# Filling up 64-row products, turning a block on TensorE, and moving weight sums to VectorE in a two-layer transformer kernel

## The chip, the cores and the metric

The kernel runs on one core of one Trainium2 chip. The core has five engines that run side by side, each with its own instruction queue: TensorE (PE, with its weight loader PEld), VectorE (DVE), ScalarE (ACT), GpSimd (POOL) and SyncE (SP, which here only issues transfers). Matrix products go from SBUF into the eight banks of PSUM, and DVE and ACT read them from there. DMA queues move data between DRAM and SBUF. The metric is device microseconds of one execution.

## The reference

Two layers, each an attention block and a gated block, on 2048 tokens of 448 features with 16 heads of 28:

```python
x = A_x
x = x + _A_ref(_layernorm(x, axis=-1), A_wqkv, A_wo)
x = x + _B_ref(_layernorm(x, axis=-1), B_w_gate, B_w_up, B_w_down)
x = x + _A_ref(_layernorm(x, axis=-1), A_wqkv, A_wo)
x = x + _B_ref(_layernorm(x, axis=-1), B_w_gate, B_w_up, B_w_down)
```

`_A_ref` is softmax attention, `(softmax(q k^T / sqrt(28)) v) wo`. `_B_ref` is `(sigmoid(x w_gate) * (x w_up)) w_down` with 1792 inner features. Both layers use the same weights. Inputs and output are float32.

## The kernel before

**Number format.** Products run on 16-bit pairs: a float32 operand is split into a high and a low float16 part, and a product is the sum of three 16-bit products (high x high, low x high, high x low). Splitting is one ACT cast (high) and one DVE subtraction (low). 448 features are three tiles of 128 rows and a tail of 64; in the tail, the high and low parts share one tile of 128 rows.

**Layer, stage by stage.** `project` makes queries, keys and values for four blocks of 512 tokens. `attend` runs the heads, `out_project` multiplies by `wo` and adds to `x`, `gated` runs the gated block. Engines follow the order in which the code issues instructions; each waits by semaphore for the tiles that it needs. SBUF tiles come from a ring of 19 large slots (`big`) and 12 quarter slots (`qrt`), first in, first out, so a new tile may wait for the last reader of an old one.

**Attention.** A unit is a score tile of 128 keys x 512 queries; a chunk is 128 keys against all 2048 queries, four units; a head has 16 chunks. Units go in groups of three: PE writes scores (L999) into three PSUM banks, ACT takes the exponential of the whole group (L1014), PE multiplies by the values two groups later (L1050) into an accumulator bank, one of two that alternate by head. At the end of a head `finish` copies the accumulator (L1076), divides and splits on DVE, and DMAs carry the result into `ot` (L1094 to L1097). A few units a head, set by `FEW` in the first layer and two otherwise, are taken from ACT: `score_aside` writes their scores into the other accumulator bank, which is free only after the previous head's copy at L1076, and DVE computes the exponential by a polynomial (nine operations, L1024 to L1033). `HeadOperands.load` loads a head's queries and keys from `qk_scr` on SP's queue; two rows of the key tile hold the constant `UNIT`, written by a DVE memset of 18 rows (L561) that comes first, and later DMAs overwrite all but two of them.

**Weights for later.** In the first layer's attention, `Prepare` reads `wo`, `w_gate`, `w_up` and `w_down`, measures them, splits them on DVE and writes the parts to DRAM (`o_parts`, `gu_parts`, `dn_parts`). Its steps are tied to chunk numbers: 12 measuring steps 4 chunks apart from chunk 6, then 5 splits 5 chunks apart, then 14 splits of gate or up weights, also 5 chunks apart. Reads, writes and the sums for the next split (`add_up`, L897) are POOL's: POOL's queue issues the DMAs, and POOL itself adds. Two large slots hold raw weights, two hold packs waiting to be written.

**Gated block.** The gate and up products use a seven-product scheme for 2 x 2 matrix halves: 256 of the features by 256 of the tokens and so on, so seven products do the work of eight. `half_steps` makes the seven moving operands of a 512-token block: four `wide` ones (two row tiles each) and three `short` ones (one row tile and a 64-row tail). In `of_halves` (L467 to L481) a wide operand gives six matmuls of 256 columns and a short one five, of which the last is over 64 rows. `gate_and_up` does one pair of inner tiles for gate and up on four PSUM banks, `chain` and `side`: 48 matmuls of wide and 30 of short operands. ACT copies the first three rounds out of the chain banks (L1278), DVE adds the side banks (L1294, L1301). The down products (`dnp`, L1247 to L1249) of the previous pair follow, 24 matmuls. An iteration is one pair of one block: 4 blocks x 7 pairs in each layer. Steps that prepare the next block are woven in by `run_fill`, one or two an iteration.

**Output projection.** `out_project` multiplies 16 token tiles by `wo` (11 matmuls each). Tiles 0 to 5 run their first nine matmuls ahead, since the last head's rows arrive late, then their last two; tiles 6 to 15 follow in bank t % 6. DVE adds each result to `x` (L1164). Between tiles the first gated block is prepared: `norm` (statistics on DVE, reciprocal root on POOL), `squares` (DVE scales and transposes in squares of 32), `store` and `gather` (the squares go to DRAM and come back with features on rows), then six empty steps, then the seven `half_steps`, the last three of which come after all tiles.

Of the kernel before, what the change touches and what calls it, by code (L numbers as in the profile page):

```python
# [13 lines left out]
F16 = mybir.dt.float16  # L14
# [5 lines left out]
P = 128  # L20
# [37 lines left out]
N_SUMS = 25  # L58
SHORT = ((10, 23, 12), (11, 24, 13), (8, 22, 9))

FEW = "1111010101"

N_SLOTS = 19
N_QUART = 12
# [38 lines left out]
def interleaved_layers(ctx: ExitStack, tc: tile.TileContext, x_in, wqkv, wo, w_gate, w_up,  # L103
# [31 lines left out]
    def bank(i, name):  # L135
        return psum(f"bank{i}", name, [P, 512])
# [100 lines left out]
    class Block:  # L237
# [10 lines left out]
        def __init__(self, b, halves=False):  # L248
            self.b = b
            self.halves = halves  # L250

        def norm(self, js=range(TB)):
            b = self.b
# [77 lines left out]
        def half_steps(self):  # L331
            def cut(k, t):

                return self.raw[:, k:k + 2, :].rearrange(
                    "p k (i t c) -> p k t i c", i=4, t=TB)[:, :, t:t + 2]

            def ordered(v):
                return v.rearrange("p k (t i c) -> p k t i c", t=2, i=4)

            def subtract(name, a, b):  # L340
                t = qrt.get(name, [P, 2, W // 2])
                a, b = [v if len(v.shape) == 5 else ordered(v) for v in (a, b)]
                for k in range(2):
                    nc.vector.tensor_tensor(ordered(t)[:, k], a[:, k], b[:, k],
                                            op=ALU.subtract)
                return t

            def divide(to, v):

                hi, lo = to[:, 0], to[:, 1]  # L350
                if len(v.shape) == 5:
                    for k in range(2):
                        nc.scalar.copy(ordered(hi)[:, k], v[:, k])
                        nc.vector.tensor_tensor(ordered(lo)[:, k], v[:, k], ordered(hi)[:, k],
                                                op=ALU.subtract)
                else:
                    nc.scalar.copy(hi, v)
                    nc.vector.tensor_tensor(lo, v, hi, op=ALU.subtract)  # L358

            def double(to):  # L360
                nc.scalar.copy(to[64:P, 0, 1], to[0:64, 0, 1])

            def r11():
                self.wide = big.get("xwide", [P, 4, 2, 2, W // 2], F16)
                self.short = big.get("xshort", [P, 3, 2, 2, W // 2], F16)
                self.t1 = subtract("t1", cut(0, 2), cut(0, 0))
                divide(self.wide[:, 0], cut(0, 0))

            def t1():
                self.t2 = subtract("t2", cut(2, 2), self.t1)  # L370
                divide(self.wide[:, 1], self.t1)
                qrt.put(self.t1)

            def t2():
                self.t3 = subtract("t3", cut(2, 2), cut(0, 2))
                divide(self.wide[:, 2], self.t2)

            def t3():
                self.t4 = subtract("t4", cut(2, 0), self.t2)
                divide(self.wide[:, 3], self.t3)  # L380
                qrt.put(self.t2, self.t3)

            def r21():
                divide(self.short[:, 0], cut(2, 0))
                double(self.short[:, 0])

            def t4():
                divide(self.short[:, 1], self.t4)
                double(self.short[:, 1])
                qrt.put(self.t4)  # L390

            def r22():
                divide(self.short[:, 2], cut(2, 2))
                double(self.short[:, 2])
                big.put(self.raw)

            return [r11, t1, t2, t3, r21, t4, r22]
# [8 lines left out]
        def begin(self):  # L406
            uid[0] += 1
            self.mv = cpool.tile([P, TB, 2], F32, name=f"mv_{uid[0]}", tag="mv", bufs=2)
            self.rs = cpool.tile([P, TB], F32, name=f"rs_{uid[0]}", tag="rs", bufs=2)
            self.xn = big.get("xn", [P, TB, D])  # L410
            self.turn_banks(4, range(4))

        def stats(self, j):
            st = cpool.tile([P, 6], F32, name=f"st_{uid[0]}_{j}", tag="st", bufs=4)
# [10 lines left out]
        def turn(self, j):  # L425
            for kt in self.pt:
                c = slice(kt * P, min((kt + 1) * P, D))
                nc.tensor.transpose(self.pt[kt][0:c.stop - c.start, j * P:(j + 1) * P],
                                    self.xn[:, j, c], ident)

        def turned_high(self):
            for kt, pt in self.pt.items():
# [34 lines left out]
    def of_halves(pm, w, blk, k, first):  # L467


        if k < 4:  # L470
            x = blk.wide[:, k]
            terms = [(w[:, i], x[:, j, t]) for t in range(2)
                     for i, j in ((2 * k + t, 0), (2 * k + t, 1), (14 + 2 * k + t, 0))]
        else:
            x = blk.short[:, k - 4]
            main, low, tail = SHORT[k - 4]
            terms = [(w[:, main], x[:, 0, 0]), (w[:, main], x[:, 1, 0]), (w[:, low], x[:, 0, 0]),
                     (w[:, tail], x[:, 0, 1]), (w[0:64, tail], x[0:64, 1, 1])]
        for i, (a, x) in enumerate(terms):
            nc.tensor.matmul(pm, a, x, start=(first and i == 0),  # L480
                             stop=(i == len(terms) - 1), skip_group_check=True)  # L481
# [64 lines left out]

    qk_scr = dpool.tile([2 * D, 2, S], F16, name="qk_scr")
    g_scr = dpool.tile([H, 2, S], F16, name="g_scr")

    class HeadOperands:  # L550

# [6 lines left out]

        def load(self):
            h, q, k = self.h, self.q, self.k  # L560
            nc.vector.memset(k[96:RG, :], UNIT)  # L561
            qs = qk_scr[h * DH:(h + 1) * DH]
            ks = qk_scr[D + h * DH:D + (h + 1) * DH]
            both = "d c n -> (d c) n"
# [22 lines left out]
    def project(layer, wq, first):  # L587
# [92 lines left out]

        def nothing():
            pass


        along = [tile0, tile1, tile2, lambda: wq.measure(2), lambda: wq.size(2), wq.split_v,
# [123 lines left out]
    class Prepare:  # L809


        def __init__(self):
            nc.vector.memset(sums[:, 3:7], 0.0)
            self.part = cpool.tile([P, 2], F32, name="part", tag="part", bufs=1)
            self.raws, self.packs = big.ring(2), big.ring(2)
            tiles = [("o", 0)] + [("d", j) for j in range(4)] + [("gu", j) for j in range(7)]
            order = [(self.measure, what) for what in tiles] + [
                (self.split, what) for what in tiles[:5] + [(w, p) for p in range(NP)
                                                            for w in ("g", "u")]]
            self.sums = self.ready_sums = None  # L820
            self.read(*tiles[0])
            self.steps = deque()
            at = 6
            for i, (do, what) in enumerate(order):
                then = order[i + 1][1] if i + 1 < len(order) else None
                self.steps.append((at, lambda do=do, what=what, then=then:
                                   self.step(do, what, then)))
                at += 4 if do == self.measure else 5
                if i == len(tiles) - 1:
                    self.steps.append((at, self.sizes))  # L830
            self.steps.append((at, self.end))
# [9 lines left out]
            big.free.extend(self.packs)  # L841

        def read(self, kind, j):
            self.next = big.at(self.raws, "raw", [P, 2048])
            if kind == "o":
                load_rows(self.view(self.next, kind), wo, 0, D, nc.gpsimd)
            elif kind == "gu":
# [25 lines left out]

        def step(self, do, what, then):
            raw = self.next
            if then:
                self.read(*then)
            self.write()
            self.sums = self.ready_sums
            if then and len(then[0]) == 1 and then[0] in "gu" and do == self.split:  # L880
                self.ready_sums = self.add_up(self.view(self.next, then[0]))
            do(raw, *what)

        def write(self):
            if self.pack:
# [3 lines left out]
        def add_up(self, v):  # L889
# [3 lines left out]
            for to, a, b, op in ((s12[:, 0], l21, l22, ALU.add),  # L893
                                 (s12[:, 1], s12[:, 0], l11, ALU.subtract),
                                 (s34[:, 0], l11, l21, ALU.subtract),
                                 (s34[:, 1], l12, s12[:, 1], ALU.subtract)):
                nc.gpsimd.tensor_tensor(to, a, b, op=op)  # L897
            return s12, s34

        def add(self, m, v):  # L900
# [24 lines left out]
        def split(self, raw, kind, j):  # L925
# [5 lines left out]
            elif kind in "gu":  # L931
                m = "gu".index(kind)
                t = big.at(self.packs, "pack", [P, N_SUMS, P], F16)
                s12, s34 = [a.rearrange("p a k n -> p (a k) n") for a in self.sums]
                for to, a in ((t[:, 0:2], v[:, 0:2, 0]), (t[:, 2:6], s12), (t[:, 6:10], s34),
                              (t[:, 10:14].rearrange("p (k z) n -> p k z n", k=2), v[:, 2:4])):
                    scaled_high(to, a, 4 + m, nc.vector)
# [4 lines left out]
                    scaled_low(to, hi, a, 4 + m)  # L942
                scaled_low(t[64:P, 9], t[0:64, 9], s34[0:64, 3], 4 + m)
                scaled_low(t[64:P, 12:14], t[0:64, 12:14], v[0:64, 3], 4 + m)
                qrt.put(*self.sums)
                self.pack = (gu_parts[j, m], t)
            else:
                n = self.count(j)
# [201 lines left out]
    def out_project(outs, gate):  # L1150
# [1 line left out]
        nc.scalar.activation(warm, warm, AF.Sigmoid)  # L1152
        nc.scalar.reg_load(gate_scale, back.bitcast(I32)[0:1, 3:4])
        first = Block(0, True)
        steps = first.steps()
        steps = deque(steps[:5] + [lambda: None] * 4 + steps[5:])
        early = 6

        def products(pm, t, kts):
# [10 lines left out]
        pms = [bank(t, "op")[:, 0:D] for t in range(early)]  # L1170
        for t in range(early):
            products(pms[t], t, range(3))
        for t in range(early):
            products(pms[t], t, [3])
            add(pms[t], t)
            if t >= TB - 1:
                run_fill(steps)
        for t in range(early, NT):
            pm = bank(t % 6, "op")[:, 0:D]
            products(pm, t, range(4))  # L1180
            add(pm, t)
            run_fill(steps)
        big.put(*outs.kt, gate.out)
        run_fill(steps, 9)
        return first
# [189 lines left out]
    keep_busy(14)  # L1375
    wq.measure(0)
    first.begin()
    first.parts()
    first.stats(0)
    first.stats(1)  # L1380
# [55 lines left out]
```

## Time and profile before

| | us |
|---|---|
| median of three runs | 2049.62 (2048.94 to 2052.22) |
| profiled execution | 2045.44 |
| its span, first to last instruction | 2043.7 |
| mean granted TensorE clock in it | 0.991 |
| TensorE / VectorE / ScalarE / GpSimd busy | 1994.4 / 1267.8 / 1324.3 / 201.8 |

Times in the profile count from the first instruction. Attention lies at about 125 to 591 and 1145 to 1593, the output projections behind each, the gated blocks at about 627 to 1039 and 1627 to 2044. The lines of the page and of the trace are quoted with the prediction. A group's line gives the busy time and the mean of one instruction, then the idle time of the engine ahead of it and what ended that. In a timeline an entry in brackets is the idle time before the instruction and its releaser. The chain of waits is followed back from the last instruction and printed in order of time: start, length, what.

### The profile page before, as it was taken

The numbers are of one execution on the slowest core, as the hardware profiler recorded it, in microseconds if no ns is written. First come the engines' busy times: TensorE is split into PE (matmuls) and PEld (weight loads), VectorE is DVE, ScalarE is ACT, GpSimd is POOL, SyncE is SP. The second block draws the span as 40 slices with busy tenths as digits, with TensorE's granted clock in tenths as the row PEclk, the third lists the DMA queues.
The fourth block names the chain that finished last, engine by engine and source line by source line (L and its number), as shares of the span: only waits on it lengthen the run. The fifth ranks groups of instructions, "written<-read, shape, count | busy, mean of one in ns | idle before, by whom it ended". The sixth has DMA issues, their size and how long they took to land. (4 is left out here: it accounts for less than half of the span.)

```text
span 2043.7 us, 53439 instructions
## 1 busy us (share of the span) xinstructions
PE 1994.4 (98%) x23405; PEld 1183.3 (58%) x23405; DVE 1267.8 (62%) x2125; ACT 1324.3 (65%) x1582; POOL 201.8 (10%) x341
## 2 busy tenths in 40 slices
PE   8999998999997999999999999999999899999999
PEld 4445554555554666666654555555555466666665
DVE  6648878877765555555465477777776654545443
ACT  5569998999953343333335799999999234343432
POOL 2013257600000000000000000000000000000000
PEclk9999998999998999999999999999999999999999
DMA  4575654521124313232234311111111532222310
GB/s 162 160 206 153 198 167 159 184 64 48 61 94 178 101 67 105 72 111 71 95 106 132 94 43 48 34 44 48 48 30 62 193 140 97 87 97 87 113 35 19
DMA packets 95029, 204.92 MB, mean 100 GB/s; under 512 B 10912, under 2 KB 61696, under 8 KB 94656
## 3 DMA queue, kind: packets, MB, share of 16 engines
q1 hardware_dynamic: 68352, 113.51, 18.1%
q0 software_dynamic: 17744, 83.50, 12.1%
q10 hardware_dynamic: 8688, 4.36, 0.8%
q8 instruction: 188, 3.08, 0.7%
q14 instruction: 57, 0.47, 0.1%
HBM read 144.18 MB, written 49.81 MB: 95 GB/s over the span
## 5 line engine op out<-in xcount | busy, mean ns | idle before, releaser
L1014 ACT ACTIVATE prob_s<-sc 128x1536 f32<-128x1536 f32 x666 | 896.0, 1538 | 14.1 <-PE sc L999 13.7
L1050 PE MATMUL acc<-prob_s,val_s 128*32 128x128 f32 (+3 forms) x7870 | 567.8, 383 | 0.0
L999 PE MATMUL sc<-qp_s 114*32 114x512 f16 x7988 | 556.5, 380 | 3.4 <-issue 1.2
L480 PEld LDWEIGHTS <-gu_s 128*128 128x128 f16 (+1 forms) x4368 | 404.2, 98 | 177.6 <-issue 93.7
L999 PEld LDWEIGHTS <-qp_s 114*32 114x32 f16 x8192 | 251.3, 95 | 240.2 <-issue 123.8
L1050 PEld LDWEIGHTS acc<-prob_s,val_s 128*32 128x32 f32 x7870 | 262.7, 110 | 159.3 <-issue 12.9
L1294 DVE TENSOR_TENSOR one_q<-side,one_q 128x512 f32<-128x512 f32 x112 | 76.6, 688 | 327.6 <-PE side L480 324.5
L480 PE MATMUL chain<-xwide_s,gu_s 128*128 128x256 f16 x2016 | 250.6, 274 | 20.1 <-ACT one_q L1278 15.9
L1278 ACT COPY one_q<-chain 128x256 f32<-128x256 f32 x224 | 82.9, 372 | 218.9 <-PE chain L480 218.8
L480 PE MATMUL side<-xshort_s,gu_s 128*128 128x256 f16 (+1 forms) x1120 | 176.1, 276 | 0.0
L1247 PE MATMUL dnp<-dn_s,hhl_q 128*128 128x448 f16 x448 | 158.4, 354 | 0.0
L1249 PE MATMUL dnp<-dn_s,hhl_q 128*128 128x448 f16 x448 | 157.9, 352 | 0.0
L1248 PE MATMUL dnp<-dn_s,hhl_q 128*128 128x448 f16 x448 | 157.9, 352 | 0.0
L465 PE MATMUL qkp<-xhl_s,wqk_s 128*128 128x512 f16 x616 | 139.6, 379 | 2.4 <-DVE xhl_s L198 0.7
L1076 DVE COPY oraw_q<-acc 128x512 f32<-128x512 f32 x32 | 22.1, 692 | 155.5 <-PE acc L1050 155.3
L1030 DVE SCALAR_TENSOR_TENSOR power_q<-power_q,expo_q 128x512 f32<-128x512 f32 x153 | 105.9, 692 | 5.2
L1078 DVE RECIPROCAL oden_q<-oden_q 128x512 f32<-128x512 f32 x32 | 107.3, 3353 | 1.1
L264 POOL TENSOR_SCALAR rs<-mv 128x4 f32<-128x4 f32 (+1 forms) x16 | 3.1, 194 | 1013.3 <-DVE mv L261 1007.3
L465 PEld LDWEIGHTS <-wqk_s 128*128 128x128 f16 x616 | 60.1, 98 | 72.0 <-issue 4.5
L480 PE MATMUL side<-xwide_s,gu_s 128*128 128x256 f16 x672 | 93.2, 275 | 1.4 <-DVE xwide_s L358 1.4
L480 PE MATMUL chain<-xshort_s,gu_s 128*128 128x256 f16 (+1 forms) x560 | 88.3, 276 | 0.0
L1278 ACT COPY two_q<-chain 128x256 f32<-128x256 f32 x112 | 41.7, 372 | 70.2 <-PE chain L480 70.2
(174 smaller groups left out, 2114.8 us busy)
## 6 DMA issues: line engine op xcount, KB each, us to landing
gu_s<-gu_parts POOLq DMA_DIRECT2D x56, 800.0 KB, 5.0
qp_s<-qk_scr SPq DMA_DIRECT2D x96, 224.0 KB
gu_s<-gu_parts SPq DMA_DIRECT2D x20, 800.0 KB
qk_scr<-qkhl_q SPq DMA_DIRECT2D x56, 256.0 KB
gu_parts<-pack_s POOLq DMA_DIRECT2D x14, 800.0 KB, 4.5
xraw_s<-xt_scr SPq DMA_DIRECT2D x14, 768.0 KB
xt_scr<-xs_s SPq DMA_DIRECT2D x38, 224.0 KB
qp_s<-qk_scr SPq DMA_DIRECT2D x64, 112.0 KB
```

The lines of the kernel that those rows point to most:

```text
L465: nc.tensor.matmul(pm, w, x, start=(i == 0), stop=(i == len(terms) - 1))
L480: nc.tensor.matmul(pm, a, x, start=(first and i == 0), stop=(i == len(terms) - 1), skip_group_check=True)
L999: nc.tensor.matmul(ps[32 * j:32 * j + 32, :], hd.k[:, keys], hd.q[:, qb * W:(qb + 1) * W], start=True, stop=True, tile_position=(0, 32 * j))
L1014: nc.scalar.activation(prob[:, 0:n, :], ps[:, 0:n, :], AF.Exp, scale=exp_scale)
L1030: nc.vector.scalar_tensor_tensor(p, p, c[k], y, op0=ALU.add, op1=ALU.mult)
L1050: nc.tensor.matmul(acc[qb * VC:(qb + 1) * VC, s], v[:, kc % TB, h, :], probs[c * NB + qb][:, s], start=(kc == 0 and a == 0), stop=(kc == N ...
L1078: nc.vector.reciprocal(den, den)
L1247: nc.tensor.matmul(pm, hl[:, 0, s], dw[:, 0, :], start=begin, stop=False)
L1248: nc.tensor.matmul(pm, hl[:, 0, s], dw[:, 1, :], start=False, stop=False)
L1249: nc.tensor.matmul(pm, hl[:, 1, s], dw[:, 0, :], start=False, stop=end)
L1278: nc.scalar.copy(to, pm)
L1294: nc.vector.tensor_tensor(one[m], side[m], one[m], op=ALU.add)
```

## The change

It has three parts.

1. The last matmul of a short operand runs over 128 rows. Rows 64 to 127 of its moving operand are zeros: the raw tile is cleared there already, and `t4`, which is a difference of differences, is cleared by a new POOL memset.
2. In `out_project`, statistics of the first four tiles follow their additions, then the four tiles are scaled. After tile 8 a new step `turn_raw` transposes them on PE into PSUM banks 4 to 7 (16 transposes), and ACT copies the banks into the raw tile, in the order of the tokens. An empty step and the `half_steps` follow, one after each tile; tiles 6 to 15 use bank t % 4. With the raw tile in this order, `half_steps` works on whole contiguous pieces. `store` and `gather` are not used for this block. `begin` no longer takes the banks, so the caller of the first layer does.
3. `add_up` runs on DVE, inside the split that uses it. Splits of gate and up weights stand 10 chunks apart, so the last comes in head 13. Their raw weights share one large slot in two halves, and the other slot goes back early. A pack is written before the next weights are read. `FEW` becomes one aside in each of the first 14 heads. The two `UNIT` rows come by DMA from a small DRAM tensor, filled once, instead of the DVE memset.

```diff
-FEW = "1111010101"
+FEW = "11111111111111"
...
             def cut(k, t):
 
+                if self.turned:
+                    return self.raw[:, k:k + 2, t * P:(t + 2) * P]
...
             def t3():
                 self.t4 = subtract("t4", cut(2, 0), self.t2)
+                nc.gpsimd.memset(self.t4[64:P, 1, :], 0.0)
...
+        def turn_raw(self):
+            self.turned = True
+            self.turn_banks(4, range(4))
+            self.raw = big.get("xraw", [P, 4, W])
+            nc.gpsimd.memset(self.raw[64:P, 3, :], 0.0)
+            for j in range(TB):
+                self.turn(j)
+            for kt, pt in self.pt.items():
+                n = P if kt < 3 else 64
+                nc.scalar.copy(self.raw[0:n, kt, :], pt[0:n])
+            big.put(self.xn)
...
-                     (w[:, tail], x[:, 0, 1]), (w[0:64, tail], x[0:64, 1, 1])]
+                     (w[:, tail], x[:, 0, 1]), (w[:, tail], x[:, 1, 1])]
...
-            nc.vector.memset(k[96:RG, :], UNIT)
+            nc.sync.dma_start(k[RQ:RG, :], unit_scr)
...
-                at += 4 if do == self.measure else 5
+                at += 4 if do == self.measure else 5 if what[0] in "od" else 10
...
+            if kind in "gu" and len(kind) == 1:
+                if self.halves is None:
+                    self.halves = big.at(self.raws, "raws", [P, 2, 1024])
+                self.next = self.halves[:, (kind == "u") * 1]
...
             raw = self.next
+            self.write()
             if then:
                 self.read(*then)
-            self.write()
-            self.sums = self.ready_sums
-            if then and len(then[0]) == 1 and then[0] in "gu" and do == self.split:
-                self.ready_sums = self.add_up(self.view(self.next, then[0]))
             do(raw, *what)
+            if what == ("g", 0):
+                big.free.append(self.raws.popleft())
...
-                nc.gpsimd.tensor_tensor(to, a, b, op=op)
+                nc.vector.tensor_tensor(to, a, b, op=op)
...
-        steps = first.steps()
-        steps = deque(steps[:5] + [lambda: None] * 4 + steps[5:])
+        steps = deque([first.turn_raw, lambda: None] + first.half_steps())
...
+        first.begin()
         for t in range(early):
             products(pms[t], t, [3])
             add(pms[t], t)
-            if t >= TB - 1:
-                run_fill(steps)
+            if t < TB:
+                first.stats(t)
+        for j in range(TB):
+            first.scale(j)
         for t in range(early, NT):
-            pm = bank(t % 6, "op")[:, 0:D]
+            pm = bank(t % 4, "op")[:, 0:D]
             products(pm, t, range(4))
             add(pm, t)
-            run_fill(steps)
+            if t >= early + 2:
+                run_fill(steps)
```

## The prediction

> **What bounds the kernel now.** I read the page's engine table first, then the windows, the groups by shape, the chain of waits in order of time, and the timeline at each place where TensorE (PE) stands still.
>
> ```profile
> span 2043.7 us, 53439 instructions
> PE 1994.4 (98%) x23405; PEld 1183.3 (58%) x23405; DVE 1267.8 (62%) x2125; ACT 1324.3 (65%) x1582; POOL 201.8 (10%) x341
> ```
>
> PE is busy for 98% of the span, so only two things can pay: time in which PE stands still or runs slowly, and busy time that a better matmul would not need. The windows (engines' busy time, granted clock, DMA share, GB/s) show where the first lies:
>
> ```profile
> 325.00:350.00 25.00, 17.97 (x280) 9.11 (x279) 21.30 (x36) 15.80 (x13) 16.67 (x27) 0.80 0.59 190
> 625.00:650.00 25.00, 14.32 (x96) 9.83 (x96) 13.76 (x30) 10.66 (x26) 0.91 (x2) 0.80 0.73 289
> 1625.00:1650.00 25.00, 14.69 (x99) 9.78 (x98) 13.42 (x29) 10.24 (x24) 1.12 (x2) 0.80 0.77 301
> 274.00:404.00 130.00, 122.96 (x2160) 65.64 (x2152) 115.42 (x182) 120.77 (x90) 88.45 (x133) 0.96 0.51 161
> 404.00:567.00 163.00, 162.20 (x2968) 95.73 (x2971) 118.34 (x170) 162.25 (x122) 1.69 (x3) 1.00 0.20 61
> ```
>
> There are three holes: one in the first layer's attention, one behind each output projection. In each the granted clock averages 0.80: 5 us of full speed missing in 25, as 10 us at half speed would give. The second kind is seen in the groups of the gated block by shape (busy, mean ns | idle before):
>
> ```profile
> L480 PEld LDWEIGHTS <-gu_s 128*128 128x128 f16 x4032 | 373.1, 98 | 106.9 <-issue 23.1
> L480 PE MATMUL side<-xshort_s,gu_s 128*128 128x256 f16 x896 | 136.1, 274 | 0.0
> L480 PE MATMUL side<-xshort_s,gu_s 64*128 64x256 f16 x224 | 62.6, 280 | 0.0
> L480 PEld LDWEIGHTS <-gu_s 64*128 64x128 f16 x336 | 31.1, 92 | 70.7 <-issue 70.7
> ```
>
> A product over 64 rows is no longer than one over 128 (280 against 274 ns), but the weight load ahead of it starts only after 70.7/336 = 0.21 us of idle loader, where a full one has 106.9/4032 = 0.03. The chain shows that PE pays for this; one gated iteration of it:
>
> ```profile
> 1662.99 1.31 PE chain L480 x12
> 1664.30 0.66 PE side L480 x6
> ...
> 1668.23 1.41 PE side L480 x10
> 1669.63 1.51 PE chain L480 x10
> 1671.14 1.51 PE side L480 x10
> ...
> 1677.30 1.31 PE chain L480 x12
> ```
>
> Twelve full products take 1.31, 0.109 each. Tens with two 64-row products among them take 1.41 to 1.51. An iteration lasts 14.31 (1662.99 to 1677.30), and its chain is PE alone.
>
> **Part 1: 64 rows filled up.** 4 blocks x 7 pairs x 2 layers x 6 products = 336. The tens of an iteration take 4.43 and would take 30 x 0.109 = 3.27, so 1.16 is lost, and a little more behind the last 64-row product, where the next line begins. By the loader's idle time it is 336 x (0.21 - 0.03) = 61 at least and 70.7 at most. I take 1.2 an iteration, nearest to the chain: 56 x 1.2 = **-67**. What could then be late is VectorE, which must have read a bank before the last ten write it:
>
> ```profile
> 1669.51 1.25 DVE L1294 TENSOR_TENSOR one_q<-side,one_q 128x512 f32<-128x512 f32 x2
> ```
>
> This is its worst iteration, with four tiles scaled and transposed first. Both additions end at 1670.76, the last ten start at 1671.14 now and about 0.8 earlier afterwards; the first of them needs only the first addition, done by about 1670.2. It fits or waits 0.2 in some seven iterations: under 2 in all. The new POOL clear of half of t4 (8 in all) stands two steps ahead of its reader on a POOL that is 10% busy: 0.
>
> A rule speaks against this part. The Trainium skill, "TensorE: Matmul & The Clock Gate", section "LDWEIGHTS (loading the stationary operand)", says that the time of a weight load follows its columns and not its rows, so filling rows would gain nothing and the sum would be 22 instead of 89. The rows agree on the duration (92 and 98 ns) and disagree on the wait in front.
>
> **Part 2: first gated block turned by PE.** The present path at the second projection, PE first, then the chain's DMA steps, then ACT:
>
> ```profile
> 1627.37 0.27 PE L480 MATMUL chain<-xwide_s,gu_s 128*128 128x256 f16 x1 [1.28 <-ACT xwide_s L353]
> 1627.98 1.37 PE L480 MATMUL chain<-xwide_s,gu_s 128*128 128x256 f16 x11 [0.35 <-DVE xwide_s L354]
> 1630.18 0.71 PE L480 MATMUL side<-xwide_s,gu_s 128*128 128x256 f16 x5 [0.72 <-DVE xwide_s L358]
> 1638.85 2.72 PE L480 MATMUL chain<-xwide_s,gu_s 128*128 128x256 f16 x12 [7.96 <-ACT one_q L1278]
> ```
> ```profile
> 1615.35 5.88 DMA xt_scr<-xs_s
> 1621.37 5.44 DMA xraw_s<-xt_scr
> ...
> 1641.57 1.21 PE side L480 x6
> ```
> ```profile
> 1636.35 0.40 ACT L361 COPY xshort_s<-xshort_s 64x256 f16<-64x256 f16 x1 [0.76 <-DVE xshort_s L358]
> ...
> 1638.43 0.65 ACT L1278 COPY one_q<-chain 128x256 f32<-128x256 f32 x2
> ```
>
> The round trip through DRAM costs 11.3 us, so the seven splitting steps run after the projection, and ACT reaches the first copy out of a chain bank (L1278) only behind them. PE waits 1.28 + 0.35 + 0.72 + 7.96 = 10.3 and then runs at half speed: 2.72 for 1.31 and 1.21 for 0.66, another 2.0. Lost: 12.3.
>
> Afterwards both DMA legs go (four stores on SP and ACT, two gathers on SP; the weight loads behind them on SP start earlier, which nobody waits for), and so do four DVE transposes; the splitting steps go as whole, contiguous operations, between tiles 10 and 15. New on PE's path, from these rows of DVE and PE:
>
> ```profile
> 1603.31 2.46 DVE L1164 SCALAR_TENSOR_TENSOR x<-op,back,x 128x448 f32<-128x448 f32 x4 [3.89 <-PE op L488]
> 1605.68 0.62 DVE L260 BATCH_NORM_STATS2 st<-x 128x6 f32<-128x448 f32 x1
> ...
> 1606.43 0.59 DVE L260 BATCH_NORM_STATS2 st<-x 128x6 f32<-128x448 f32 x1
> ```
> ```profile
> 1605.00 0.35 PE L490 MATMUL op<-wout_s,ot_s 128*128 128x448 f16 x1
> ...
> 37.03 1.04 PE L428 MATMUL turn<-ident,xn_s 128*128 128x128 f32 x8
> ```
>
> (a) Statistics now stand between the additions, 0.75 each beside 0.61 for an addition, and tile 6 uses bank 2 instead of 0. It is free after three additions and two statistics: 1603.31 + 1.83 + 1.50 = 1606.64, where PE is ready at 1605.00. PE waits 1.65. (b) Sixteen transposes, eight in 1.04: 2.1. Their inputs (four scalings, done near 1612) are ready before tile 8 ends near 1613. (c) The last splits still stand ahead of L1278: behind PE's last product an addition and a subtraction on DVE (0.2 + 0.61 + 0.69), then what now takes 1636.35 to 1638.81, 2.46; of these 3.95, PE fills 18 x 0.109 = 1.96. PE waits 2.0. Together 5.75, so 12.3 - 5.75 = 6.55 a layer: **-13.1**. Bounds for both layers: -17 if (c) is covered, -3 if half speed comes back in both.
>
> **Part 3: weights' sums, asides, units.** The hole in the attention:
>
> ```profile
> 335.40 0.60 DVE L203 TENSOR_SCALAR pack_s<-raw_s,up 128x256 f16<-128x256 f32 x1 [2.94 <-DMA gu_parts<-pack_s]
> ...
> 343.70 0.62 PE L999 MATMUL aside<-qp_s 114*32 114x512 f16 x4 [7.03 <-DVE oraw_q L1076]
> ```
> ```profile
> 346.57 1.45 ACT L1014 ACTIVATE prob_s<-sc 128x1536 f32<-128x1536 f32 x1 [8.09 <-PE sc L999]
> 349.13 12.34 ACT L1014 ACTIVATE prob_s<-sc 128x1536 f32<-128x1536 f32 x9 [1.11 <-PE sc L999]
> ...
> 406.39 6.90 ACT L1014 ACTIVATE prob_s<-sc 128x1536 f32<-128x1536 f32 x5 [0.60 <-PE sc L999]
> ```
>
> PE's scores for VectorE (the aside) need the other accumulator bank, and the copy that frees it (L1076) stands behind weight splits on DVE, themselves waiting for a pack buffer. It costs 8.09 + 1.11 + 0.60 = 9.8. In 274 to 404 DVE is busy for 115.42 of 130. With 10 chunks between splits, is that still so? Prices:
>
> ```profile
> L1030 DVE SCALAR_TENSOR_TENSOR power_q<-power_q,expo_q 128x512 f32<-128x512 f32 x153 | 105.9, 692 | 5.2
> L561 DVE MEMSET qp_s<- 18x2048 f16 x32 | 56.5, 1765 | 22.9 <-issue 13.8 <-DMA qp_s<-qk_scr 4.5 <-DMA qp_s<-g_scr 4.1
> L344 DVE TENSOR_TENSOR t_q<-xraw_s 128x256 f32<-128x256 f32 x32 | 12.1, 418 | 13.4 <-DMA xraw_s<-xt_scr 13.4
> ```
>
> From 404 on, ACT does 122 groups in 163 us, 1.34 each, so a head (62 to 64 tiles, three to a group) takes about 28. With two asides a head and nearly no split, DVE has 118.34/163 x 28 = 20.3 of it. An aside is nine operations of up to 0.69, some 6: one fewer gives 14.3, without the memset 12.5. A split costs about 5 and its four sums, now on DVE, 4 x 0.42 = 1.7; 1.6 a head add 10.7. So 23.2 of 28, 83%, and never two splits in a row; the pack buffer is 17 us old when it is wanted. The copy is then late by one split at most, and the aside comes five chunks (8.7 us) later. The hole goes: -9.8, and one aside less in all (18 for 19) gives a third of a group of 1.37 us (12.34/9) back to ACT: **-9.3**, bounds 0 and -11. Writing ahead of reading on POOL's queue makes reads wait for the previous split, which is long done. The units' DMA adds one issue on SP to each of 32 heads and takes a wait for DVE's memset (1.77) off the same queue: 0, and no more than 1.8 either way at the start of each attention, the one place where PE waits for a head's load.
>
> **Sum.** 67 + 13.1 + 9.3 = 89. The profiled execution took 2045.44 (span 2043.7), 0.2% below the median 2049.62, on which I put the forecast: **1960**.
>
> **Rivals.** *Rows don't matter* (a): the wait belongs to the place in the sequence, part 1 gives nothing: 2049.6 - 22 = 2027. For it: equal durations. Against it: the other 4032 loads at the same line don't wait. *Half speed returns* (b) because waits (a) and (c) stay in the projection: 5 us a layer, about 1970. *The hole stays* (c) since DVE's work moves rather than shrinks: 1969. *Slower* (d): the two halves of one raw buffer are ordered as one tile, so each split waits for the read just issued into the other half, and DVE passes this on to the accumulator's copy in every head. Price: a hole like today's, 9.8, for each; it decides from ten holes on, and 14 splits would give 137 - 89 = 48 more: 2097. Against it: today's tiles are read part by part without such waits.
>
> A wait of 2 us leaves the clock alone by the Trainium skill, "TensorE: Matmul & The Clock Gate", Part 1, which asks for an idle window of about 3.4 us before half speed; the trace shows half speed behind 7 and 8 us.
>
> **Numbers.** Forecast 0.70, (b) or (c) 0.16, (a) or part of it 0.07, (d) 0.04, no effect 0.03. The likeliest case has 1949 to 1972; with (b) and (c) the range reaches 1980. Under 0.2%, 4 us, a measurement of this kernel can't be told from no change: faster 0.93, within 0.02, slower 0.05.
>
> **What shows it.** No 64x128 load at the product line, tens at 1.09, iterations at 13.1. PE's last product of a projection and the first chain product back to back, one wait near 2 before the second round, clock 1.00 in all windows. No wait of an aside over 1 us. Wrong if tens stay at 1.5, if a clock of 0.8 remains, or if DVE waits for raw reads.

## The result, and the profile after

| | before | after |
|---|---|---|
| median | 2050.92 (2048.94 to 2054.26) | 1953.05 (1952.52 to 1955.52) |
| ratio after/before, 95% interval | | 0.9524 [0.9507, 0.954] |
| profiled execution | 2045.44 | 1955.52 |
| its span | 2043.7 | 1953.8 |

The change takes 97.9 us off the medians and 89.9 off the two profiled spans. The page after, span and engine table:

```profile
span 1953.8 us, 53508 instructions
PE 1924.3 (98%) x23469; PEld 1215.3 (62%) x23469; DVE 1187.5 (61%) x2117; ACT 1321.3 (68%) x1585; POOL 164.0 (8%) x306
```

TensorE has 64 instructions more and 70 us less to do. Where the time went is read by cutting both timelines at the first and last product of each kind:

```
us, from the starts of PE's products        before    after   change   price in the prediction
attention 0 (first score to projection)     465.52   458.98    -6.5    -9.3
projection 0, first to last product          33.28    36.80    +3.5 \
last product to first chain product           2.51     0.19    -2.3  | part 2: -6.55 a layer
first gated iteration                        21.38    10.70   -10.7 /
27 other gated iterations, layer 0          390.79   357.72   -33.1    -32.4 (27 x 1.2)
projection 1, gap, first iteration: change      +3.6 - 1.4 - 10.4 = -8.2
27 other gated iterations, layer 1: change      -33.2
everything else                                  under 0.5 each
```

Part 1 took 66.3/54 = 1.23 off an iteration, the two first ones included 68.8; less that, part 2 gave 8.2 + 7.0 = 15.2; part 3 gave 6.5 here.

The loader's group at the product line, where 64x128 loads had their own row before:

```profile
L499 PEld LDWEIGHTS <-gu_s 128*128 128x128 f16 x4368 | 427.1, 98 | 64.3 <-issue 4.9
```

All 4368 loads have one shape and 0.015 us (64.3/4368) of idle loader each, where 336 of them had 0.21. One iteration in PE's timeline:

```profile
1618.16 1.47 PE L499 MATMUL chain<-xwide_s,gu_s 128*128 128x256 f16 x12
...
1623.40 1.25 PE L499 MATMUL side<-xshort_s,gu_s 128*128 128x256 f16 x10
1624.49 1.26 PE L499 MATMUL chain<-xshort_s,gu_s 128*128 128x256 f16 x10
1625.58 1.25 PE L499 MATMUL side<-xshort_s,gu_s 128*128 128x256 f16 x10
...
1631.21 1.47 PE L499 MATMUL chain<-xwide_s,gu_s 128*128 128x256 f16 x12
```

Tens follow each other at 1.09, where they took up to 1.51, and the iteration lasts 13.05. Behind the second projection:

```profile
1558.41 0.35 PE L509 MATMUL op<-wout_s,ot_s 128*128 128x448 f16 x1 [1.78 <-DVE x L1194]
...
1580.77 0.35 PE L507 MATMUL op<-wout_s,ot_s 128*128 128x448 f16 x1
1580.96 1.48 PE L499 MATMUL chain<-xwide_s,gu_s 128*128 128x256 f16 x12
1582.27 0.82 PE L499 MATMUL side<-xwide_s,gu_s 128*128 128x256 f16 x6
1585.12 1.47 PE L499 MATMUL chain<-xwide_s,gu_s 128*128 128x256 f16 x12 [2.03 <-ACT one_q L1312]
```

The first chain product follows 0.19 behind the last of the projection. Both waits that the prediction put into the new path are there: (a) for the bank at tile 6, priced 1.65, found 1.78 (in the first layer 1.20, plus 0.42 for the head's rows just before), and (c), priced 2.0, found 2.03.

Windows of the profiled execution after (busy PE, PEld, DVE, ACT, POOL, then clock, DMA share, GB/s):

```profile
125.00:150.00 25.00, 21.40 (x316) 10.54 (x319) 6.89 (x12) 19.06 (x16) 1.36 (x3) 0.93 0.94 275
274.00:404.00 130.00, 130.00 (x2356) 73.60 (x2352) 103.37 (x185) 129.89 (x98) 26.53 (x46) 1.00 0.41 120
404.00:567.00 163.00, 163.00 (x2968) 91.46 (x2967) 116.05 (x201) 162.93 (x122) 18.62 (x32) 1.00 0.31 96
```

The hole of the attention is gone: PE fills all of 274 to 404, at full clock. But in the start of the attention, 125 to 150, PE is idle for 3.6 us, where it was idle for 2.0 before the change. The row:

```profile
128.88 1.26 PE L1030 MATMUL sc<-qp_s 114*32 114x512 f16 x18 [2.50 <-issue]
```

PE waits 2.50 for nothing that the profile shows, and half speed follows. The prediction had the units' DMA at 0 at just this place. So there were three questions for the chip: does each part do what it was priced at, what is it about 64 rows, and what took the hole away and made the start longer?

### The profile page after: what moved, and what is told of

It is laid out like the page before. It is cut to its first block, busy times and chain, and to the rows that moved or that the text cites. A ratio compares the mean times of both kernels' runs of the same rounds, so it can differ in the third digit from the quotient of the medians.

```text
span 1953.8 us, 53508 instructions
## 1 busy us (share of the span) xinstructions
PE 1924.3 (98%) x23469; PEld 1215.3 (62%) x23469; DVE 1187.5 (61%) x2117; ACT 1321.3 (68%) x1585; POOL 164.0 (8%) x306
## 5 line engine op out<-in xcount | busy, mean ns | idle before, releaser
L1081 PE MATMUL acc<-prob_s,val_s 128*32 128x256 f32 (+3 forms) x7902 | 567.6, 381 | 0.0
L499 PEld LDWEIGHTS <-gu_s 128*128 128x128 f16 x4368 | 427.1, 98 | 64.3 <-issue 4.9
L1328 DVE TENSOR_TENSOR one_q<-side,one_q 128x512 f32<-128x512 f32 x112 | 71.9, 683 | 305.4 <-PE side L499 305.4
L499 PE MATMUL side<-xshort_s,gu_s 128*128 128x256 f16 x1120 | 140.9, 273 | 0.0
L650 ACT ACTIVATE qkhl_q<-qkp 128x512 f16<-128x512 f32 x56 | 33.3, 594 | 62.9 <-PE qkp L484 62.8
L1339 ACT ACTIVATE one_q<-one_q 128x512 f32<-128x512 f32 x56 | 35.3, 630 | 59.8 <-DVE one_q L1328 59.8
```

Source lines behind the costliest of these rows:

```text
L499: nc.tensor.matmul(pm, a, x, start=(first and i == 0), stop=(i == len(terms) - 1), skip_group_check=True)
L1081: nc.tensor.matmul(acc[qb * VC:(qb + 1) * VC, s], v[:, kc % TB, h, :], probs[c * NB + qb][:, s], start=(kc == 0 and a == 0), stop=(kc == N ...
L1328: nc.vector.tensor_tensor(one[m], side[m], one[m], op=ALU.add)
```

## The experiments

**Each part alone**, the three of them added to the kernel before, and the kernel before itself once more as yardstick (the kernel before has a median of 2048.94 beside them, 2042.88 to 2052.12).

Part 1 alone:

```diff
-                      (w[:, tail], x[:, 0, 1]), (w[0:64, tail], x[0:64, 1, 1])]
+                      (w[:, tail], x[:, 0, 1]), (w[:, tail], x[:, 1, 1])]
...
+                nc.gpsimd.memset(self.t4[64:P, 1, :], 0.0)
```

> The kernel before with part 1 alone: the last product of a short operand over 128 rows, and t4 cleared in its lower half. Theory (a load over fewer rows is not made ahead of time): every gated iteration goes from 14.31 to 13.05 us, 56 iterations, so 68 to 70 us less than before, about 1981; the holes behind both output projections and in the first attention stay. Rival (the wait belongs to the place in the sequence): iterations stay at 14.31 and the time at 2050. Rival (the parts help one another, since the changed kernel gained 98 by the medians and 90 by the profiled executions): clearly less than 68.

Measured: 1980.06, ratio 0.9665 [0.9644, 0.9686], 69 us. The two stretches of 27 iterations fell by 33.07 and 33.24, as in the full change. That settles the size of part 1.

Part 2 alone:

```diff
-        steps = first.steps()
-        steps = deque(steps[:5] + [lambda: None] * 4 + steps[5:])
+        steps = deque([first.turn_raw, lambda: None] + first.half_steps())
...
+            if t < TB:
+                first.stats(t)
...
-            pm = bank(t % 6, "op")[:, 0:D]
+            pm = bank(t % 4, "op")[:, 0:D]
```

> The kernel before with part 2 alone: first gated block turned by TensorE. Theory: both holes behind the projections shrink from 12.3 to about 5 us of lost time, clock 1.00 there, so 13 to 16 us less, about 2036; the hole in the first attention and iterations of 14.31 stay. Rival (the preparation was hidden by what surrounds it): within 4 us of before.

Measured: 2036.42, ratio 0.9941 [0.992, 0.9961], 12.5 us. In its trace the projections grew by 3.5 each, the gaps and first iterations fell by 11.8 and 10.6: 15.2 together, as in the full change.

Part 3 alone (with the halves of the raw slot and the write ahead of the read, as in the full diff):

```diff
-FEW = "1111010101"
+FEW = "11111111111111"
...
-            nc.vector.memset(k[96:RG, :], UNIT)
+            nc.sync.dma_start(k[RQ:RG, :], unit_scr)
...
-                at += 4 if do == self.measure else 5
+                at += 4 if do == self.measure else 5 if what[0] in "od" else 10
...
-                nc.gpsimd.tensor_tensor(to, a, b, op=op)
+                nc.vector.tensor_tensor(to, a, b, op=op)
```

> The kernel before with part 3 alone: sums on VectorE, splits 10 chunks apart, one aside a head, units by DMA. Theory: no wait of an aside over 1 us, so 9.8 us less in the middle of the first attention, but a longer start of it as in the changed kernel (2.50 us of PE without a releaser and 3.4 us at half speed instead of 1.16 us): 6 us less in all, about 2044. Rival (the long start comes from something else in the changed kernel): start as before, 9 to 10 us less, about 2041. Rival (the hole only moves): within 4 us of before.

Measured: 2042.19, ratio 0.9967 [0.9952, 0.9982], 6.8 us. This is near the 6 of the theory, but by luck, since its reason is not in the profile: PE's wait at the start of the first attention is 1.01, without half speed behind it. The first attention took 455.78. The second projection of queries, keys and values took 3.7 longer than the yardstick's: there, ahead of the other attention, PE waited on "issue", and half speed went with it:

```profile
1135.92 0.53 PE L491 MATMUL vp<-wv_s,xhl_s 128*128 128x448 f16 x1 [3.19 <-issue]
```

The yardstick:

> The kernel before, unchanged, for a second profile. The first profiled execution took 2045.44 us, the other runs 2048.94 to 2054.26. If single executions of this kernel differ because half-speed stretches start at another moment in its holes, the clock's stretches of half speed will be longer or more in an execution that takes longer; if the difference lies elsewhere, the three stretches of 10.24 us stay and another stage is longer.

Measured: 2049.46, ratio 0.9998 [0.9985, 1.0012]. All stages agree with the first profile of the kernel before within 0.6, but for the start (1.5 shorter) and the first attention: 471.01 instead of 465.52. ACT's timeline shows why:

```profile
344.92 1.45 ACT L1014 ACTIVATE prob_s<-sc 128x1536 f32<-128x1536 f32 x1 [8.07 <-PE sc L999]
...
409.78 1.45 ACT L1014 ACTIVATE prob_s<-sc 128x1536 f32<-128x1536 f32 x1 [6.28 <-PE sc L999]
```

The second hole cost 0.60 in the execution on which the prediction was built. It is 6.28 here, 6.62 and 6.38 in the profiles of part 1 and part 2 alone, and 6.21 and 4.24 in those of the two experiments on 64 rows below: the first profile was the exception. Of the expected theories neither fits whole: the first hole has 6.83 at half speed here, not 10.24, and the second has 6.83 of its own. From 471.01 to the 455.78 of part 3 alone, the attention is 15.2 shorter, where the hole was priced at 9.8.

**The changed kernel again**, nothing edited.

> The changed kernel once more, nothing altered, as the yardstick of this group and for a second profiled execution. Theory A (the longer start of the first attention, 2.50 us before the second group of scores and 3.41 us at half speed behind it, comes from this edit): both are there again, PE busy 21 to 22 of the 25 us from 125 to 150. Theory B (they belong to one execution): the wait is near 1.0 as in the runs of the kernel before (1.16, 1.01), PE busy 23 to 24 and no half speed. Either way 1950 to 1956, with the attention of the second layer at 463 to 466.

Measured: 1951.51, ratio 0.9523 [0.9504, 0.9542]; first attention 456.38.

```profile
126.16 1.26 PE L1030 MATMUL sc<-qp_s 114*32 114x512 f16 x18 [1.13 <-issue]
```
```profile
125.00:150.00 25.00, 23.40 (x395) 12.43 (x396) 10.60 (x17) 22.91 (x18) 1.26 (x3) 1.00 0.92 271
```

Theory B: the wait is 1.13, as before the change (1.16, 1.01), and the clock stays up. The wait of 2.50 did not come again. Half speed at this place did, in two profiles of edits below that don't touch the loads of a head: behind a wait of 1.97 in the kernel before with products over 96 rows, which still fills the units on VectorE, and behind one of 1.17 in the changed kernel with one more empty step.

**The units' DMA undone** in the changed kernel:

```diff
-            nc.sync.dma_start(k[RQ:RG, :], unit_scr)
+            nc.vector.memset(k[96:RG, :], UNIT)
```

> The changed kernel with VectorE's fill of the two unit rows (1.77 us a head) in place of their DMA. Theory A (the units' DMA delays the first head's operands): the start of the first attention gets 2 to 4 us shorter, the clock stays at 1.00 there, total 2 to 4 less than the changed kernel run beside it. Theory B (it is not the DMA): the start stays as it is. For the rest of the attention: VectorE gets 1.77 more in 28 us a head, 25.0 for 23.2 by my estimate; below 28 no aside should wait, 0 change; if the copy out of the accumulator is late in a head, up to 5 us more.

Measured: 1953.45, beside 1951.51. The first attention took 455.65, 0.7 less than with the DMA; VectorE had 113.80 instead of 106.30 in 274 to 404, and no aside waited. So in the attention the units' DMA neither costs nor gains anything that shows. The 1.9 us in the medians has its like at another place of the profile, the first gated iteration of layer 0:

```profile
622.16 2.65 PE L499 MATMUL chain<-xwide_s,gu_s 128*128 128x256 f16 x12 [2.03 <-ACT one_q L1312]
624.60 1.35 PE L499 MATMUL side<-xwide_s,gu_s 128*128 128x256 f16 x6
```

The same wait of 2.03 as after, but half speed behind it: 12.38 for the iteration instead of 10.71. All four runs are slower than the four of the changed kernel beside them, with a clock of 0.998 for 0.999, so each may have had such a stretch; that was not seen, nor why.

**Five chunks between splits**, with all else of part 3 kept:

```diff
-                at += 4 if do == self.measure else 5 if what[0] in "od" else 10
+                at += 4 if do == self.measure else 5
```

> The changed kernel with five chunks between two weight splits of the gated layer, as before, instead of ten; the sums stay on VectorE and the write of a pack stays ahead of the next read on GpSimd's queue. Theory A (the spacing took the hole away): a split with its sums is 6.7 us for every 8.7, with an aside more than VectorE has; one or two holes of 5 to 9 come back in the first attention, 8 to 17 more than the changed kernel, the aside waiting for the copy out of the accumulator. Theory B (the queue took it away: before, a pack was written to memory behind GpSimd's sums and four reads, now ahead of them): no wait for a pack's write on VectorE, holes of 0 to 2, within 3 of the changed kernel.

Measured: 1965.49, ratio 0.959 [0.957, 0.961], 14 us more than the changed kernel beside it; first attention 468.58. PE's timeline, and the windows:

```profile
313.01 0.40 PE L1030 MATMUL aside<-qp_s 114*32 114x512 f16 x4 [3.83 <-DVE oraw_q L1107]
344.94 0.40 PE L1030 MATMUL aside<-qp_s 114*32 114x512 f16 x4 [1.85 <-DVE oraw_q L1107]
375.55 0.50 PE L1030 MATMUL aside<-qp_s 114*32 114x512 f16 x4 [2.43 <-DVE oraw_q L1107]
```
```profile
300.00:330.00 30.00, 26.17 (x449) 15.64 (x444) 28.22 (x55) 24.94 (x20) 10.26 (x17) 0.94 0.54 169
330.00:360.00 30.00, 28.14 (x516) 15.57 (x512) 28.21 (x58) 28.26 (x22) 13.97 (x23) 1.00 0.54 176
360.00:390.00 30.00, 27.57 (x476) 15.20 (x472) 29.34 (x59) 26.23 (x21) 10.00 (x18) 0.94 0.55 161
```

VectorE (the third time of a row) has 28 to 29 us of work in 30, and the copy out of the accumulator is late in one head after another. The three waits come to 8.1, and the two stretches at half speed behind the first and the third cost 1.7 each; theory A expected fewer and longer holes, but its time is met. No split waits for a pack's write any more, so theory B was right about the queue, and it doesn't help. Without the wider spacing the hole is back.

**The sums back on GpSimd**, one split ahead as before, with the spacing kept:

```diff
-                nc.vector.tensor_tensor(to, a, b, op=op)
+                nc.gpsimd.tensor_tensor(to, a, b, op=op)
...
+            self.sums = self.ready_sums
+            if then and len(then[0]) == 1 and then[0] in "gu" and do == self.split:
+                self.ready_sums = self.add_up(self.view(self.next, then[0]))
```

> The changed kernel with the four sums of a weight split back on GpSimd, made one split ahead as before; the spacing of ten chunks and the write ahead of the read stay. Theory A (the spacing took the hole away): no aside waits over 1 us and the ratio to the kernel before stays at 0.952. Theory B (the sums' place did): holes of 5 to 8 in the first attention, ratio 0.956 to 0.960.

Measured: 1952.83, ratio 0.9528 [0.9508, 0.9549]; first attention 455.88, no aside waits. Theory A: moving the sums to VectorE is worth nothing here.

**What a product over 64 rows costs.** First, each of them issued twice in a row, in the kernel before:

```diff
-                      (w[:, tail], x[:, 0, 1]), (w[0:64, tail], x[0:64, 1, 1])]
+                      (w[:, tail], x[:, 0, 1]), (w[0:64, tail], x[0:64, 1, 1]),
+                      (w[0:64, tail], x[0:64, 1, 1])]
```

> The kernel before with each product over 64 rows issued twice in a row (the product of the low part with the tail is so added twice). Theory A (a load of 64 rows is not made ahead, each pays): 336 more at 0.109 + 0.205, 105 more, about 2155; a group of now twelve takes 2.1 to 2.2. Theory B (the change between 64 and 128 rows is what is paid): 336 more at 0.109, 37 more, about 2087; a group of twelve takes 1.73.

Then the same product over 96 rows:

```diff
-                      (w[:, tail], x[:, 0, 1]), (w[0:64, tail], x[0:64, 1, 1])]
+                      (w[:, tail], x[:, 0, 1]), (w[0:96, tail], x[0:96, 1, 1])]
...
+                nc.gpsimd.memset(self.t4[64:P, 1, :], 0.0)
```

> The kernel before with the last product over 96 rows instead of 64 (rows 64 to 95 filled with zeros). Theory A (any load of fewer than 128 rows pays): tens stay at 1.51, total 2050. Theory B (only a load that stays in the lower half pays): tens at 1.09, total 1980, ratio 0.966.

Measured: twice 2089.01, ratio 1.0192 [1.0163, 1.0221]; 96 rows 1983.47, ratio 0.9677 [0.965, 0.9705]. The loads, first with the product issued twice, then over 96 rows:

```profile
L481 PEld LDWEIGHTS <-gu_s 64*128 64x128 f16 x672 | 37.0, 94 | 70.7 <-issue 70.7
```
```profile
L481 PEld LDWEIGHTS <-gu_s 96*128 96x128 f16 x336 | 32.6, 97 | 4.0
```

Twice as many loads, and the same 70.7 us of waiting: the second of two 64-row loads is free. An iteration grew from 14.31 to 14.96, 0.108 for each of its six more products, what any product takes. (The other 3 of the 39 us lie elsewhere: this profile has an "issue" wait of 4.17 ahead of the second attention.) And 96 rows wait no more than 128 (4.0/336 = 0.012). So the price is neither per load nor for "fewer than 128 rows": it is paid where the row count changes between 128 and 64.

It is paid both ways. The return to 128 rows, in the kernel before, and the loads of 128 rows with the product issued twice:

```profile
1669.35 0.28 PE L480 MATMUL side<-xshort_s,gu_s 64*128 64x256 f16 x1
1669.56 1.58 PE L480 MATMUL chain<-xshort_s,gu_s 128*128 128x256 f16 x10
```
```profile
L481 PEld LDWEIGHTS <-gu_s 128*128 128x128 f16 x4032 | 373.1, 98 | 132.4 <-issue 82.0
```

From start to start, PE takes 0.109 from one product over 128 rows to the next, 0.205 to one over 64, 0.119 from 64 to 64, and 0.21 from 64 back to 128. That is 0.10 for each of the two changes, 0.20 for the pair; 336 pairs come to 67 of the 68.8 us. The loader's idle time is no measure of it: ahead of the 128-row loads, "issue" rose from 23.1 to 82.0 with the product issued twice, and the price of a pair stayed at 0.20.

**The two new waits taken out** of the changed kernel, which is also the better version:

```diff
-        steps = deque([first.turn_raw, lambda: None] + first.half_steps())
+        steps = deque([first.turn_raw] + first.half_steps())
...
-            pm = bank(t % 4, "op")[:, 0:D]
+            pm = bank((t - early) % 4, "op")[:, 0:D]
```

> The changed kernel with two waits of the output projection attacked: tile 6 takes the accumulator bank that was emptied first instead of the third, and the empty step before the splits is left out, so that they start a tile earlier. If the two waits cost what they were priced at (1.65 and 2.0 in each of two projections), 7.3 less than the changed kernel beside it; if only the bank counts, 3.3; if the statistics on VectorE set the end of the projection whatever the bank, 0 to 1.

Measured: 1945.18, ratio 0.9492 [0.9471, 0.9514]: 6.3 under the changed kernel beside it. In the traces each projection is 1.94 shorter and each first iteration 1.79, 7.5 together, near the 7.3 expected; part of it is lost at other places of this profile, such as a start of the attention 1.4 later. What is left of (c), in layer 0:

```profile
618.88 1.47 PE L499 MATMUL chain<-xwide_s,gu_s 128*128 128x256 f16 x12 [0.24 <-ACT one_q L1312]
```

**One more empty step**, the opposite:

```diff
-        steps = deque([first.turn_raw, lambda: None] + first.half_steps())
+        steps = deque([first.turn_raw, lambda: None, lambda: None] + first.half_steps())
```

> The changed kernel with one more empty step ahead of the splits of the first gated block, so that the wait before the second round grows from 2.03 by one split, to between 3.3 and 4.5. Theory A (half speed needs a window of 3.41 us with little work in it, which a wait of 2.03 leaves to chance): half speed stands behind the wait in both layers, and the first gated iteration goes from 10.71 to between 13.5 and 15; 6 to 9 us more in all, ratio 0.955 to 0.957. Theory B (only waits of 7 and 8 us, as seen before, bring it): 10.71 + 1.3 to 2.5, 12.0 to 13.2, clock 1.00, 3 to 5 us more, ratio 0.9535 to 0.955.

Measured: 1958.86, ratio 0.9557 [0.9535, 0.9578]; the first iterations took 14.13 and 14.18. PE's timeline, layer 0 then layer 1:

```profile
625.37 2.72 PE L499 MATMUL chain<-xwide_s,gu_s 128*128 128x256 f16 x12 [3.83 <-ACT one_q L1312]
...
1587.32 2.22 PE L499 MATMUL chain<-xwide_s,gu_s 128*128 128x256 f16 x12 [3.83 <-ACT one_q L1312]
```

Theory A: 1.8 more of waiting, and half speed in both layers for another 1.6 each.

## Why the prediction was right, and where its sizes were off

The forecast was 1960, the time 1953.05, with 97.9 gained for 89 worked out. The mechanism of parts 1 and 2 was right, that of part 3 in half; three terms were small.

- **Part 1, -67: gained 68.8.** Tens at 1.09 and iterations of 13.05 are as forecast. It was 1.23 an iteration, not 1.2. The 1.2 came from PE's chain, the sound measure, which had "a little more behind the last 64-row product": that little is a return to 128 rows. The bounds 61 and 70.7 from the loader's idle time hold by luck, as the product issued twice shows. The feared wait for the side addition is 0.17 in the seven iterations that also scale and transpose four tiles (13.22), 1.2 us in all.
- **Part 2, -13.1: gained 15.2.** The new costs held: (a) 1.20 and 1.78 for 1.65, (b) with (a) 3.5 a projection for 3.75, (c) 2.03 for 2.0. The term that was too small is "Lost: 12.3", taken for both layers. It was read at the second projection (a gap of 1.63 and an iteration of 21.08); the first lost more, 2.51 and 21.38.
- **Part 3, -9.3: 6.5 in the attention between the first profiles, 14.6 between the second ones.** "It costs 8.09 + 1.11 + 0.60 = 9.8" is the mis-sized term: the second hole is 4.2 to 6.6 in the five other profiles that still have it. By medians, part 3 alone gave 6.8, since its profile loses time ahead of the second attention. The units' DMA at 0 held; the 2.50 at the start came in one of two profiles of the same kernel. The reason was half right: VectorE is as busy as worked out (103.37 of 130 in 274 to 404, 80%, for 83%), and without the wider spacing it is not (124.30). The sums could have stayed on GpSimd.
- With 68.8 + 15.2 + 14.6 (471.01 to 456.38), the three come to 98.6, for 97.9 measured.
- Rival (a) is out by the first experiment, (c) by the windows, (d) by the absence of any aside's wait. Rival (b), half speed after the waits of the projection, did not show in the changed kernel; in two profiles of edits that leave this place alone it did, for 1.7 in one layer, not 5 in each.

"A wait of 2 us leaves the clock alone" is wrong as a rule. Twelve waits of 2.03 stand in the traces of part 2 alone, of the changed kernel (two profiles), and of the three kernels that left this place as it was: half speed followed two of them, and both of the waits of 3.83 that one more empty step made. Each of these four stretches lasted 3.41 us. At the start of the first attention, with other short waits near it, even one of 1.17 was followed by such a stretch. The Trainium skill, "TensorE: Matmul & The Clock Gate", Part 1, has a free-running window of that length and so a loss that varies from run to run; the traces agree (stretches of 3.41, behind 2 of 12 like waits). They also show that a wait well under the window's length can be enough.

The section "LDWEIGHTS (loading the stationary operand)" of that page of the Trainium skill, which spoke against part 1, says that a load's time goes by its columns; the traces agree (92 to 98 ns for 64, 96 and 128 rows). What part 1 removed is another thing, 0.10 us at each change of the row count between 128 and 64, and it was 69 us of this kernel.

**Open.** The single parts give 69 + 12.5 + 6.8 = 88 by their medians, ten less than all three together. Part 3 alone lost 3.7 + 1.7 around the "issue" wait of 3.19 in its profile; whether each of its runs did wasn't seen. These waits, 0.87 to 4.17 us near the start of an attention, have no releaser in the profile; the DMA engines are busy for 67 to 100% during them. That PE then waits for its own program is a guess, and wasn't tested. Why a change of the row count costs PE 0.10 us is not shown, and neither is why the second hole differs between executions. The new `FEW` and the write ahead of the read were not tried by themselves, so it is not shown that the spacing would take the hole away without them.

## What to carry to other kernels

Look at the idle time ahead of a weight load by shape, not at the load's duration, and then at the starts of the products for the price: here, mixing 64 rows into 128 cost more than the rows it saved, and mixing in 96 cost almost nothing (iterations of 13.08 for 13.05). Before pricing a hole from one profile, see in a second one whether it is always the same size. And when a queue's work is late, work out its load over one period of the pattern: here, moving the sums to another engine without spreading the splits left PE waiting, and spreading them without moving the sums took it away.

## What the hardware showed that I had not expected

Beside the price of a change between 128 and 64 rows and the clock after short waits, told above: some VectorE operations take longer beside GpSimd. At the yardstick's second hole, with a sum on GpSimd at the same time, a split's operation takes double:

```profile
399.30 0.47 DVE L208 SCALAR_TENSOR_TENSOR pack_s<-raw_s,up,pack_s 128x256 f16<-128x256 f32 x1
...
401.36 0.94 DVE L208 SCALAR_TENSOR_TENSOR pack_s<-raw_s,up,pack_s 128x256 f16<-128x256 f32 x1
```
```profile
401.10 0.92 POOL L897 TENSOR_TENSOR sums_q<-sums_q,raw_s 128x256 f32<-128x256 f32 x1
```

With the sums back on GpSimd, one of an aside's operations (`power_q` from `power_q` and `expo_q`) takes 0.86 on average in 274 to 404, with them on VectorE 0.69. It makes VectorE later in the kernel before; whether it decides between a hole of 0.6 and one of 6.3 is not shown.
